# All tiles of u and 13 groups of x turned by DMA transposes in a fused attention and phase-mixing kernel

## The chip, the cores and the metric

One core of one Trainium2 chip runs the kernel. A core has five engines with a queue of their own each: TensorE (PE), VectorE (DVE), ScalarE (ACT), GpSimd (POOL) and SyncE (SP), which only issues DMAs here. Transfers run on 16 DMA engines. The metric is device time in microseconds (us) of one execution, as the median of three runs.

## The reference

Inputs are q, k and v of shape (8, 8, 576, 64): batch, heads, sequence, head dimension. The sequence is cut into nine chunks of 64, and attention runs inside a chunk only. Its output x, (8, 576, 512), goes through a phase layer:

```python
scores = scale * np.matmul(q_c, k_c.transpose(0, 1, 2, 4, 3))      # per chunk of 64
attn = softmax(scores)
x = np.matmul(attn, v_c)                     # to (8, 576, 512), heads side by side
theta = x @ w_theta                          # 512 x 512
zr, zi = x * cos(theta), x * sin(theta)
y = einsum('ts,bsd->btd', w_tok_r, zr) + einsum('ts,bsd->btd', w_tok_i, zi)   # 576 x 576 each
u = x + y
out = u + np.maximum(u @ w_ch, 0.0)          # w_ch 512 x 512, float32
```

## The kernel before

The eight batches are taken in four pairs (0 to 3). A pair has nine tiles of 128 tokens: four of its first batch, four of its second, and one, the middle tile, that holds the last 64 tokens of both. So there are 36 tiles, numbered 00 to 38 in the order by pair and tile (the pair's digit, then 0 to 8). Loads and attention work in groups: A and B are tiles 0, 1 and 2, 3 of the pair's first batch, C and D the same of the second, M is the middle tile alone. Every group but M has two tiles.

The whole program is one list, ORDER, of steps such as `W.02.0`: kind, pair with group or tile, and a slot (a PSUM bank, or the number of a buffer). The steps are emitted in that order, and each engine runs its own instructions in the order in which they were emitted; the engines keep apart only by semaphores where data or a buffer requires it. So a step's place in the list fixes only what stands before it on its own engine. The kinds are:

- `qk`, `v`, `lw`, `lc`: loads that GpSimd issues and that cast to float16 on the way (q and k of a group, v of a group, one block of both token matrices, w_ch). `hq`, `hk`, `lt`: loads in float32 that SyncE issues, with a cast by `cqa`, `ckv`, `cta`. q, k and the weights land in 13 `land` buffers; v lands in `v16`, which holds two pairs.
- `T`, `Tq`, `Tk`, `Tk0`, `Tk1` (VectorE): turn q and k in 32 by 32 blocks. `S` (TensorE): scores. `E` (ScalarE): exp. `V0`, `V1` (TensorE): attention times v, four heads each. `N0`, `N1` (VectorE): division, which writes x.
- `X` (TensorE, through PSUM) with `xa` or `xv` (a copy by ScalarE or VectorE), or `xd` alone (a DMA transpose that SyncE issues): x turned, which `H` needs. `H` (TensorE): theta. `G` (ScalarE): cos and sin. `Z` (VectorE): zr and zi.
- `TW` with `twv` or `twa`: one block of the token matrices turned. `Y`, or in parts `Ya`, `Yb`, `Ym` (TensorE): the mix of all nine tiles of a pair into one output tile. `A` (VectorE): u = x + y, written over x.
- `U` (TensorE, through PSUM) with `ua` or `uv`, or `ud` alone (a DMA transpose that SyncE issues): u turned, which `W` needs. `W` (TensorE): u times w_ch. `R` (VectorE): relu and sum. `st`, `sa`: the store, issued by SyncE or by ScalarE.
- `dm.n.b`: n matmuls on zeros in the early part, with no use of their result.

A transposing matmul of `X` is line 419 and one of `U` line 539, four for each tile; the DMA transposes are line 436 (`xd`) and line 547 (`ud`). The mix is line 522, theta line 457, W line 562, scores line 339, attention line 382, the block transpose of VectorE line 321. An `xd` of a two-tile group moves 256 KB, one of an M group and a `ud` 128 KB. The transposed tiles of u go through eight `uT` buffers and those of x through four `xT` buffers; a DMA transpose waits on SyncE's queue until its input is written and the last reader of its buffer is done, and what stands behind it on that queue waits with it.

Of the kernel before, what the change touches and what calls it, by code (L numbers as in the profile page):

```python
# [65 lines left out]


@with_exitstack
def kernel(
# [86 lines left out]
    def dummies(n, b):  # L156
        for _ in range(n):
            nc.tensor.matmul(banks(b), zeros[:, 0:P], zeros)

    def load_qk(p, g, slot):
# [3 lines left out]
        for w, ap in enumerate((q, k)):  # L166
            if bb is None:
                for b in range(2):
                    nc.gpsimd.dma_start(
                        t[quarter[b], w].rearrange("p h s d -> p h (s d)"),  # L170
                        ap[2 * p + b, :, s0:S, :].rearrange("h (p s) d -> p h (s d)", s=2),
                    )
            else:
                nc.gpsimd.dma_start(  # L174
                    t[:, w].rearrange("p h s d -> p h (s d)"),
                    ap[2 * p + bb, :, s0 : s0 + GT, :].rearrange(
                        "h (p s) d -> p h (s d)", s=2
                    ),
                )
# [55 lines left out]
    def cast_v(engine):  # L235
        def cast(p, g):
            slot = (p % 2) * NT + GROUPS[g][0]
# [421 lines left out]
```

## Time and profile before

| | |
|---|---|
| three runs | 193.11, 193.46, 195.17 us; median 193.46 |
| the profiled execution | 192.63 us, span 190.9 us |
| granted TensorE clock | 0.999 |
| busy: PE, DVE, ACT, POOL | 179.3, 136.8, 100.7, 84.9 us |
| loads by GpSimd | 15.49 MB as landed, in 75152 packets, last issue at 107.33 us |
| DMA transposes | 18 of u, 7 of x; the first issued at 104.68 us |

The time is that of the whole execution; the span is from the first to the last instruction in the trace, and the traced times count from its start. A busy matmul is no proof of a full array, since matmuls are pipelined: a 128x512 one takes 379 ns from start to end, and they follow each other every 216 ns. In the DMA view a line of a queue gives its packets, its megabytes, and the summed time of its packets as a share of 16 engines' time; the packets of one engine overlap, so the share can pass 100%.

### The profile page before, as it was taken

What the parts mean: (1) busy time and instruction counts of PE and PEld (TensorE: products, weight loads), DVE (VectorE), ACT (ScalarE), POOL (GpSimd) and SP (SyncE); (2) the same over time, 40 slices, a digit from 0 to 9 for tenths busy, and PEclk for the clock granted to TensorE, in tenths of its full rate; (3) what the DMA queues carried; (4) which work ended last, traced back from release to release, by engine and by line L of the source; (5) the groups of instructions that cost most, each with busy time, mean ns of one, the idle gap of its engine ahead of it and who ended that gap; (6) DMA issues with size and microseconds to landing.
All of it is one profiled execution on the core that took longest, in us unless ns stands there. A gap on an engine that the chain in (4) does not pass through costs nothing.

```text
span 190.9 us, 6053 instructions
## 1 busy us (share of the span) xinstructions
PE 179.3 (94%) x2626; PEld 93.0 (49%) x2626; DVE 136.8 (72%) x254; ACT 100.7 (53%) x129; POOL 84.9 (44%) x119
## 2 busy tenths in 40 slices
PE   7769899999999999998999999999989999999980
PEld 2245555655556555655456555454544444444430
DVE  0167889789958989959788798967771963672761
ACT  3238979399579780499062774996344650000000
POOL 7786988559856997789578400000000000000000
PEclk9999999999999999999999999999999999999999
DMA  5999999999999999999999998632498315256596
GB/s 156 252 225 187 176 172 174 193 132 159 259 199 162 120 162 198 183 173 194 201 228 200 176 163 180 85 86 82 84 87 177 99 55 137 59 192 165 133 319 213
DMA packets 99867, 31.48 MB, mean 165 GB/s; under 512 B 90880, under 2 KB 94848, under 8 KB 99840
## 3 DMA queue, kind: packets, MB, share of 16 engines
q0 software_dynamic: 75152, 15.49, 93.9%
q1 hardware_dynamic: 21936, 10.75, 24.8%
q10 hardware_dynamic: 2752, 4.85, 7.4%
q8 instruction: 20, 0.33, 0.7%
q14 instruction: 7, 0.06, 0.1%
HBM read 33.06 MB, written 9.44 MB: 223 GB/s over the span
## 4 chain that ended last, share of the span: by engine, by line
PE 64%; DMA 17%; POOL 6%; ACT 5%; DVE 3%; issue 3%; DVEq 0%; POOLq 0%
PE psum L522 29%; DMA land<-in_k_dram 15%; PE psum L562 12%; PE psum L457 11%; PE psum L339 4%; POOL v L214 3%; PE psum L382 2%; POOL land L174 2%; DMA uT<-x 2%; PE psum L419 2%; PE psum L539 2%; ACT L144 1%; PE psum L288 1%; DVE T L321 1%; ACT sin L476 1%
## 5 line engine op out<-in xcount | busy, mean ns | idle before, releaser
L522 PEld LDWEIGHTS <-wT 128*128 128x128 f16 (+1 forms) x360 | 31.0, 100 | 34.5 <-issue 1.2
L214 POOL DMA_DIRECT2D v<-in_v_dram x56 | 42.0, 772 | 7.1 <-DMA land<-in_k_dram 4.0
L522 PE MATMUL psum<-zr,wT 128*128 128x512 f16 (+1 forms) x180 | 44.7, 380 | 0.0
L522 PE MATMUL psum<-zi,wT 128*128 128x512 f16 (+1 forms) x180 | 42.9, 379 | 0.0
L534 DVE TENSOR_TENSOR x<-psum,x 128x512 f16<-128x512 f32 x36 | 24.3, 684 | 20.2 <-PE psum L522 20.0
L562 PE MATMUL psum<-wch,uT 128*128 128x512 f16 (+1 forms) x148 | 35.2, 374 | 1.2 <-DMA uT<-x 0.7
L457 PE MATMUL psum<-wtheta,xT 128*128 128x512 f16 x144 | 34.1, 379 | 0.2 <-DVE xT L442 0.2
L321 DVE STREAM_TRANSPOSE T<-land 128x1024 f32<-128x1024 f32 (+4 forms) x27 | 25.4, 953 | 10.0 <-DMA land<-in_q_dram 5.9
L574 DVE SCALAR_TENSOR_TENSOR o<-psum,x 128x512 f32<-128x512 f32 (+1 forms) x37 | 24.1, 670 | 9.3 <-PE psum L562 9.2
L365 ACT ACTIVATE eT<-psum 128x1024 f16<-128x1024 f32 (+1 forms) x22 | 18.2, 860 | 22.7 <-PE psum L339 20.3
L476 ACT ACTIVATE cos<-psum,pihalf 128x1024 f16<-128x1024 f32 (+1 forms) x22 | 21.1, 958 | 12.5 <-PE psum L457 11.4
L399 DVE TENSOR_TENSOR x<-psum,recip 128x512 f16<-128x512 f32 (+1 forms) x40 | 25.5, 638 | 1.4
L144 ACT ACT_TABLE_LOAD x20 | 25.7, 1283 | 1.1 <-PEq L643 0.7
L562 PEld LDWEIGHTS <-uT 128*128 128x128 f16 x148 | 13.6, 98 | 15.8 <-DMA uT<-x 1.5
L457 PEld LDWEIGHTS <-xT 128*128 128x128 f16 x144 | 13.5, 98 | 16.0 <-DVE xT L442 0.6
L476 ACT ACTIVATE sin<-psum 128x1024 f16<-128x1024 f32 (+1 forms) x22 | 19.0, 865 | 0.0
L174 POOL DMA_DIRECT2D land<-in_q_dram x15 | 14.3, 950 | 5.8 <-DMA land<-in_k_dram 2.1
L339 PE MATMUL psum<-T 32*64 32x64 f16 x1152 | 13.7, 193 | 3.3 <-DVE T L321 3.3
L339 PEld LDWEIGHTS <-T 32*64 32x64 f16 x1152 | 11.8, 106 | 7.6 <-DVE T L321 4.3
L174 POOL DMA_DIRECT2D land<-in_k_dram x15 | 13.6, 907 | 1.7 <-DMA land<-in_k_dram 1.5
L492 DVE TENSOR_TENSOR zr<-x,cos 128x1024 f16<-128x1024 f16 (+1 forms) x18 | 11.2, 623 | 1.3 <-ACT cos L476 1.0
L493 DVE TENSOR_TENSOR zi<-x,sin 128x1024 f16<-128x1024 f16 (+1 forms) x18 | 11.3, 627 | 0.8 <-ACT sin L476 0.7
(39 smaller groups left out, 124.9 us busy)
## 6 DMA issues: line engine op xcount, KB each, us to landing
...
v<-in_v_dram POOLq DMA_DIRECT2D x40, 64.0 KB, 6.4
...
```

The source lines that it names most:

```text
L144: nc.scalar.activation(out=first, in_=pihalf, func=func)
L174: nc.gpsimd.dma_start(t[:, w].rearrange("p h s d -> p h (s d)"), ap[2 * p + bb, :, s0 : s0 + GT, :].rearrange("h (p s) d -> p h (s d)", s=2),)
L214: nc.gpsimd.dma_start(v16[rows, slot + t, :, 0:D], v[b, :, t0 : t0 + m, :].rearrange("h s d -> s h d"),)
L321: nc.vector.transpose(to.bitcast(FP32).rearrange("p (x l s) -> p x s l", l=32, s=2), src.bitcast(FP32).rearrange("p (x s d) -> p x s d", s ...
L339: nc.tensor.matmul(ps[half[r ^ cc], r, h - hs[0]], t[quarter[c], 1, h, :, e], t[quarter[c], 0, h, :, e], start=(e == 0), stop=(e == 1), ti ...
L399: nc.vector.tensor_tensor(out=x.rearrange("p r (h d) -> p r h d", h=H // 2), in0=ps[:, :, :, 0:D], in1=recip[:, 0:n].broadcast_to((P, n, H ...
L457: nc.tensor.matmul(ps[:, (j - js[0]) * DM : (j - js[0] + 1) * DM], xT[:, j, a, :], wtheta16[:, a, :], start=(a == 0), stop=(a == NDB - 1),)
L476: nc.scalar.activation(out=t[:, js[0] : js[-1] + 1].rearrange("p j e -> p (j e)"), in_=ps, func=AF.Sin, bias=bias, scale=1.0,)
L522: nc.tensor.matmul(ps[half[c]] if j == MID else ps, wT[:, kt, t0 : min(t0 + P, S)], z, start=(b is not None and i == 0), stop=(i == len(kt ...
L534: nc.vector.tensor_tensor(out=x, in0=st.pop(("ps_y", p, j)), in1=x, op=ALU.add)
L562: nc.tensor.matmul(ps, uT[:, a, :], wch16[:, a, cols[f]], start=(a == 0), stop=(a == NDB - 1),)
L574: nc.vector.scalar_tensor_tensor(out=o, in0=ps, scalar=0.0, in1=st["x", p][:, j, cols[f]], op0=ALU.max, op1=ALU.add,)
```

## The change

The list ORDER is another one. All 36 tiles of u are turned by `ud`, where 18 were turned by `U` with a copy; 13 of the 20 groups of x are turned by `xd` (1A, 1M, 1C, 2A, 2B, 2M, 2C, 2D and all of pair 3), where seven were. The loads, the stores and all other steps stand in another order, the first group is 0A, whose q and k SyncE loads, and there are 42 dummy matmuls instead of 32. Of the 49 DMA transposes 19 stand in the list ahead of `V1.2D`, the first use of the 42nd of the 45 loads of that list.

Around it, the places of the tiles in x, zr, zi and v16 are worked out by new helpers (`place`, `pairs`, `places`, `middle`), which with the constants given (`WITH_NEXT` empty, `OWN` zero) leave each step one pair's group and the same number of instructions as before, and the tile of zeros shrinks to 128 columns, with the dummies' moving operand broadcast from one column.

```diff
 ORDER = """
-pre.00 qk.0M.0 hq.0A.1 cqa.0A.2 hk.0A.3 Tq.0M.0 Tk.0M v.0M init.00 v.0A dm.21.7 S.0M.0
-E.0M.0 lw.02.4 qk.0B.5 dm.3.7 V1.0M.1 lw.01.6 v.0B ckv.0A lw.00.7 qk.0C.8 Tq.0A.1 Tk0.0A
-Tk1.0A dm.1.7 S0.0A.2 S1.0A.4 E0.0A.1 lw.03.9 v.0C qk.0D.10 v.0D E1.0A lc.00 qk.1A.11
-v.1A N1.0M dm.1.7 V0.0A.6 N0.0A V0.0M.0 V1.0A.1 N1.0A dm.3.5 TW.02.3 lt.00.12 X0.0A.5
-lt.01.1 twv.02 X1.0A.6 xv0.0A.0 cta.01 xv1.0A cta.00 dm.2.7 H0.0A.7 Tq.0B.2 Tk0.0B
-Tk1.0B N0.0M H1.0A.1 S1.0B.2 G0.0A.0 G1.0A Z0.0A dm.1.7 S0.0B.4 Z1.0A TW.01.6 X.0M.0
-Ya.02.1 xv.0M.1 twv.01 E0.0B.2 V0.0B.4 N0.0B qk.1M.0 E1.0B V1.0B.6 N1.0B H.0M.0 Ya.01.2
-X0.0B.3 X1.0B.4 TW.00.5 xv0.0B.2 G.0M.1 xa1.0B H0.0B.7 H1.0B.0 Tq.0C.0 G0.0B.2 G1.0B
-Tk.0C S.0C.3 twv.00 Ya.00.7 Z0.0B TW.03.5 Z1.0B Z.0M Yb.02 Ym.02 E.0C.3 Yb.00 Ym.00 A.02
-Yb.01 Tq.0D.1 V1.0C.3 twa.03 A.00 V0.0C.0 Ym.01 Ya.03.5 Tk.0D N1.0C S.0D.6 U.02.3 N0.0C
-ua.02.0 qk.1B.3 Yb.03 v.1M lw.04.2 X.0C.4 A.01 U.01.0 Ym.03 qk.1C.1 U.00.1 v.1B E.0D.0
-A.03 V1.0D.2 N1.0D ua.01.1 qk.1D.4 qk.2M.12 v.1D V0.0D.6 xa.0C.3 v.2D qk.2C.5 v.1C
-W.02.0 N0.0D H.0C.4 U.03.2 ua.00.2 G.0C.0 T.1A.2 W.00.3 R.00.0 X.0D.1 S.1A.6 xv.0D.0
-E.1A.1 v.2B qk.2A.6 W.01.3 H.0D.4 v.2M V0.1A.6 R.02.1 V1.1A.0 R.01.2 Ym.07.3 uv.03.3
-G.0D.2 Ym.06.2 Z.0C N1.1A Ya.07 Ym.04.0 Ya.04 Ya.06 N0.1A W.03.1 X.1A.6 xa.1A.1 Z.0D
-Yb.06 T.1M.0 Yb.04 TW.04.4 R.03.3 twa.04 T.1B.1 S.1M.7 st.02 E.1M.2 A.04 A.06 S.1B.0
-Yb.07 H.1A.4 V1.1M.6 qk.3M.7 qk.2B.8 v.2A A.07 N1.1M E.1B.3 V1.1B.2 st.01 V0.1B.0 N0.1B
-Y.08.7 V0.1M.6 N1.1B G.1A.1 U.06.0 ua.06.4 Ym.05.1 N0.1M X.1B.4 st.00 U.04.5 Ya.05
-U.07.2 X.1M.3 xa.1B.2 A.08 T.1D.2 xv.1M.3 ua.04.5 H.1B.6 H.1M.0 v.3A qk.3A.9 ua.07.6
-W.07.4 qk.3B.10 T.1C.0 G.1B.0 v.2C S.1C.2 S.1D.5 U.08.7 Yb.05 Z.1A Z.1B G.1M.2 Z.1M
-uv.08.7 R.07.4 Y.12.0 E.1D.0 Y.11.7 v.3M A.12 E.1C.1 A.05 qk.3C.11 V0.1D.4 T.2M.1
-V1.1D.2 V0.1C.0 Y.13.6 N1.1D W.08.2 N0.1D U.12.3 N0.1C A.11 X.1D.4 R.08.5 st.03 uv.12.0
-T.2A.0 Y.10.5 A.10 A.13 V1.1C.0 S.2M.7 v.3C qk.2D.0 S.2A.2 N1.1C U.11.5 st.07 uv.11.2
-W.06.6 st.08 X.1C.0 W.04.1 xa.1D.0 H.1D.4 E.2A.3 E.2M.2 R.04.1 U.05.2 xa.1C.1 T.2B.2
-G.1D.1 H.1C.0 uv.05.1 T.2C.1 W.05.3 Z.1D st.04 R.05.2 S.2B.4 V1.2M.7 G.1C.0 Z.1C V0.2M.2
-E.2B.0 sa.05 N1.2M W.11.3 U.10.0 ua.10.3 Y.17.1 N0.2M R.11.0 R.06.3 A.17 Y.15.7 V0.2B.4
-V0.2A.2 A.15 N0.2B N0.2A V1.2B.0 Y.18.6 A.18 S.2C.4 sa.11 X.2M.7 xv.2M.2 W.10.2 N1.2B
-R.10.4 E.2C.1 T.3M.0 H.2M.3 Y.16.6 U.13.7 G.2M.2 X.2B.4 V1.2A.0 A.16 st.06 st.10 uv.13.6
-xa.2B.3 V0.2C.2 V1.2C.5 N1.2A N1.2C N0.2C W.13.7 R.13.5 sa.13 X.2A.4 xd.2C.0 xv.2A.1
-H.2B.0 U.18.5 U.17.6 U.16.2 uv.16.7 U.15.3 Y.14.7 ua.18.4 T.2D.2 Z.2M ua.17.5 ua.15.1
-W.16.4 H.2A.5 G.2B.1 S.3M.2 S.2D.0 Z.2B G.2A.0 W.12.3 E.3M.2 R.16.1 A.14 Z.2A U.14.4
-W.18.7 R.12.2 R.18.0 Y.21.5 Y.23.6 E.2D.0 st.18 V0.2D.2 T.3C.1 A.21 ua.14.2 v.3B T.3A.0
-V1.2D.0 qk.3D.3 N1.2D N0.2D T.3B.2 sa.12 S.3A.4 W.14.7 sa.16 A.23 xd.2D.2 H.2C.0 E.3A.3
-R.14.3 Y.22.4 G.2C.2 V0.3M.5 V1.3M.2 T.3D.0 A.22 Z.2C N1.3M st.14 S.3B.6 E.3B.1 S.3C.0
-H.2D.3 E.3C.0 N0.3M W.15.6 Y.20.7 v.3D G.2D.1 ud.23.3 R.15.4 V0.3B.0 V0.3A.5 V1.3A.2
-Z.2D A.20 W.17.4 R.17.5 N0.3B Y.24.7 Y.27.4 N1.3A N0.3A A.27 V1.3B.0 xd.3M.3 N1.3B st.15
-A.24 V1.3C.2 N1.3C S.3D.5 Y.28.4 V0.3C.0 ud.20.6 E.3D.2 V0.3D.5 V1.3D.2 A.28 H.3M.7
-N0.3C N0.3D N1.3D xd.3A.1 G.3M.0 ud.27.7 W.27.4 Y.25.0 xd.3B.0 H.3A.5 A.25 ud.22.0
-Y.26.1 G.3A.2 H.3B.2 ud.21.4 st.17 A.26 R.27.0 xd.3C.2 G.3B.1 H.3C.5 Z.3A W.21.7 xd.3D.3
-Z.3M ud.24.2 G.3C.2 Z.3B R.21.2 Z.3C H.3D.0 Y.33.4 W.24.2 Y.31.3 sa.21 R.24.1 A.33
-G.3D.0 Z.3D Y.32.5 st.27 Y.34.6 A.34 Y.36.7 st.24 ud.25.1 W.25.0 A.32 A.36 ud.33.5
-W.33.1 ud.26.7 R.33.3 W.20.2 W.23.4 W.26.6 A.31 R.23.4 R.25.5 ud.32.4 W.32.5 Y.30.7
-sa.23 R.20.0 Y.38.1 Y.35.3 ud.34.2 sa.25 R.26.2 R.32.1 W.34.4 A.30 sa.20 A.35 st.26
-ud.28.1 ud.36.5 W.28.0 R.34.4 ud.30.6 ud.35.3 A.38 W.30.2 R.30.5 R.28.0 Y.37.6 A.37
-sa.33 W.35.5 ud.31.7 ud.38.4 R.35.2 sa.30 sa.28 sa.34 W.36.7 R.36.3 ud.37.2 sa.35 sa.36
-W.31.3 R.31.5 W.38.4 R.38.0 W.22.1 R.22.4 sa.31 sa.32 sa.22 W0.37.2 R0.37.2 W1.37.0
-st.38 R1.37.3 sa1.37 st0.37
+pre.00 hq.0A.0 hk.0A.1 cqa.0A.2 ckv.0A Tq.0A.0 Tk0.0A dm.23.7 S0.0A.0 Tk1.0A lt.00.3
+lt.01.4 init.00 v.0A qk.0M.5 E0.0A.0 S1.0A.2 E1.0A cta.01 dm.3.7 V1.0A.4 cta.00 N1.0A
+V0.0A.6 N0.0A dm.8.3 X0.0A.0 X1.0A.1 Tq.0M.1 xv0.0A.0 xa1.0A qk.0B.6 dm.1.7 H0.0A.2 v.0M
+Tq.0B.2 v.0B H1.0A.3 Tk.0M Tk1.0B S.0M.4 lw.02.7 qk.0C.8 E.0M.1 S1.0B.5 lw.00.9 Tk0.0B
+S0.0B.0 E0.0B.2 V0.0M.7 E1.0B N0.0M dm.1.4 V1.0M.4 N1.0M dm.1.1 V1.0B.0 N1.0B dm.1.7
+X.0M.7 xv.0M.1 G0.0A.0 V0.0B.5 G1.0A N0.0B lw.03.10 dm.2.4 TW.02.0 Z1.0A dm.1.7 X0.0B.4
+xv0.0B.2 X1.0B.7 xa1.0B H.0M.2 Z0.0A v.0C H1.0B.5 H0.0B.6 Tq.0C.0 twa.02 G.0M.1 Tk.0C
+dm.1.7 S.0C.3 Z.0M qk.0D.11 G0.0B.2 G1.0B Z0.0B Z1.0B Ya.02.7 TW.00.0 TW.03.5 twv.03
+twv.00 Yb.02 Ym.02 Ya.03.2 E.0C.3 Ym.07.5 V1.0C.3 N1.0C Tq.0D.1 V0.0C.0 Ya.00.6 Yb.00
+Tk.0D S.0D.3 E.0D.0 Ym.00 N0.0C A.02 A.00 X.0C.0 xa.0C.3 v.0D lw.01.12 Yb.03 qk.1A.0
+V0.0D.3 V1.0D.6 Ym.03 N0.0D N1.0D H.0C.0 X.0D.3 xv.0D.0 TW.01.6 H.0D.3 qk.1M.1 G.0C.0
+A.03 T.1A.2 S.1A.0 twa.01 Ya.01.2 T.1M.0 Z.0C S.1M.6 G.0D.1 E.1M.1 Ym.06.7 Yb.01 E.1A.2
+qk.1B.2 v.1M Ya.07 Z.0D Yb.07 v.1A V0.1A.3 V1.1A.0 qk.1C.4 v.1B T.1B.1 N1.1A lw.04.3
+A.07 lc.00 Ya.06 qk.1D.5 V1.1M.6 Yb.06 N1.1M S.1B.0 N0.1A Ym.05.5 Ya.05 E.1B.3 Ym.01
+Ym.04.6 A.01 v.2A V0.1M.3 qk.3M.6 V0.1B.0 N0.1B T.1C.2 ud.00.0 N0.1M ud.03.1 v.1C v.1D
+qk.2A.7 Ya.04 qk.3C.8 v.2M Yb.04 A.04 qk.2M.9 qk.2B.10 qk.2D.11 v.2B ud.02.2 Yb.05
+V1.1B.0 N1.1B A.06 ud.07.3 W.00.4 W.03.2 X.1B.3 xa.1B.1 R.03.0 qk.3A.12 v.2C qk.2C.0
+v.3M S.1C.0 W.07.6 T.1D.0 qk.3B.1 R.07.1 E.1C.0 v.3A W.02.7 TW.04.2 H.1B.0 v.3B v.2D
+R.02.2 xd.1A.2 A.05 G.1B.2 twv.04 H.1A.6 R.00.3 T.3M.1 xd.1M.3 H.1M.5 Y.08.2 Z.1B G.1A.0
+sa.03 Z.1A ud.01.4 sa.02 V0.1C.3 V1.1C.0 st.07 G.1M.1 Z.1M S.1D.6 Y.10.5 N0.1C A.08 A.10
+E.1D.2 N1.1C Y.12.3 T.2A.2 V1.1D.6 st.00 V0.1D.4 N1.1D N0.1D Y.11.2 A.11 A.12 W.01.0
+R.01.4 ud.04.5 Y.13.1 S.2A.6 E.2A.1 X.1D.4 v.3D T.2M.0 S.2M.5 A.13 S.3M.2 V0.2A.0 N0.2A
+V1.2A.6 xa.1D.0 ud.08.6 N1.2A xd.1C.1 H.1D.3 G.1D.2 ud.06.7 H.1C.0 W.04.6 ud.05.0 W.08.7
+G.1C.0 E.3M.3 W.05.3 ud.10.1 ud.12.3 T.2B.2 S.2B.0 ud.13.2 Z.1D R.04.5 Z.1C W.10.4
+R.05.1 Y.14.6 T.2D.0 sa.04 R.10.3 E.2B.0 sa.05 V0.2B.2 N0.2B sa.10 V1.2B.0 E.2M.2 N1.2B
+V0.2M.4 st.01 Y.15.5 Y.17.2 R.08.0 V1.2M.3 Y.16.0 A.15 N0.2M A.17 N1.2M T.2C.1 A.16
+W.12.1 T.3A.2 A.14 R.12.2 S.2C.4 E.2C.1 sa.12 Y.18.7 A.18 xd.2A.2 V0.2C.2 xd.2B.3 T.3C.1
+V1.2C.4 S.2D.0 E.2D.0 H.2A.6 N0.2C T.3B.0 H.2B.0 qk.3D.2 N1.2C G.2A.1 xd.2M.0 H.2M.2
+Z.2A G.2B.2 Z.2B G.2M.0 Z.2M W.06.3 W.13.4 ud.14.4 W.14.5 R.14.5 v.3C S.3B.6 R.13.4
+V1.2D.0 Y.22.2 R.06.1 N1.2D E.3B.2 Y.23.5 st.08 V0.3B.6 V1.3B.3 A.22 sa.13 ud.16.5
+T.3D.0 V0.2D.0 N0.2D Y.21.2 N0.3B A.23 Y.20.0 W.16.1 A.20 R.16.3 xd.2C.1 H.2C.6 st.06
+xd.2D.2 H.2D.0 G.2C.1 ud.11.6 N1.3B A.21 Z.2C W.11.5 G.2D.2 R.11.2 ud.15.0 W.15.3 Z.2D
+S.3D.6 S.3A.4 S.3C.0 Y.26.2 E.3C.1 A.26 st.16 Y.25.0 A.25 R.15.0 E.3A.2 V0.3A.4 st.14
+Y.28.1 N0.3A ud.21.1 ud.23.3 ud.18.7 sa.15 ud.17.2 A.28 V0.3C.2 V1.3C.4 st.11 E.3D.0
+ud.22.4 N0.3C ud.25.5 V1.3A.6 N1.3A W.23.0 W.18.1 R.18.4 R.23.1 N1.3C xd.3A.3 xd.3B.0
+W.17.2 Y.27.3 A.27 R.17.3 V1.3M.6 V1.3D.0 V0.3D.4 N0.3D st.18 ud.26.6 V0.3M.7 W.21.3
+R.21.5 N0.3M sa.21 N1.3M Y.24.2 st.17 H.3B.4 G.3B.0 A.24 N1.3D xd.3C.1 Z.3B W.25.3
+R.25.2 H.3A.6 ud.27.0 W.26.2 G.3A.1 xd.3M.2 H.3M.0 Z.3A G.3M.2 st.25 H.3C.4 W.22.1 Z.3M
+Y.31.3 xd.3D.0 H.3D.6 Y.30.0 G.3C.0 G.3D.1 Z.3C Z.3D A.30 Y.33.4 R.22.0 ud.28.3 A.31
+Y.36.5 A.33 Y.38.6 Y.32.7 A.36 A.38 W.28.0 Y.35.1 Y.34.3 st.23 ud.24.7 R.28.4 ud.33.2
+A.32 W.33.4 ud.31.1 sa.22 ud.20.5 ud.36.6 W.36.5 A.35 A.34 ud.38.4 W.38.6 R.33.3 sa.28
+sa.33 ud.30.3 R.36.5 sa.36 ud.35.2 R.38.2 W.30.0 R.30.1 W.31.7 R.26.0 Y.37.1 W.35.3
+sa.38 ud.34.6 A.37 st.30 R.31.4 W.34.4 R.34.3 sa.31 W.27.5 R.35.5 W.20.6 R.27.2 R.20.1
+ud.32.4 sa.26 W.24.0 sa.34 W.32.2 R.24.4 ud.37.3 sa.20 W0.37.1 W1.37.7 sa.24 R.32.0
+R0.37.3 sa.32 st.35 R1.37.5 sa1.37 st.27 st0.37
 """.split()
+
+
+
+WITH_NEXT = ()
+OWN = 0
...
-    zeros = const.tile([P, DM], FP16, name="zeros")
+    zeros = const.tile([P, P], FP16, name="zeros")
...
     st = {}
     for name in ("x", "zr", "zi"):
-        t = const.tile([P, 2 * NT, DM], FP16, name=name)
-        for p in range(NP):
-            st[name, p] = t[:, p % 2 * NT : (p % 2 + 1) * NT]
+        st[name] = const.tile([P, 2 * NT + OWN, DM], FP16, name=name)
+
+    def place(p, j):
+        return p % 2 * MID + j if j < MID else 2 * MID + (1, 0, 1, 2 * OWN)[p]
+
+    def pairs(p, g):
+        if g != "M":
+            return [p]
+        ps = [p, p + 1] if p in WITH_NEXT else [p]
+        return sorted(ps, key=lambda x: place(x, MID))
...
-            nc.tensor.matmul(banks(b), zeros[:, 0:P], zeros)
+            nc.tensor.matmul(banks(b), zeros, zeros[:, 0:1].broadcast_to((P, DM)))
...
             if engine == "d":
                 nc.sync.dma_start(
                     xT.rearrange("p j a c -> p (j a) c"),
-                    st["x", p][:, j0 + js[0] : j0 + js[-1] + 1].rearrange("p j d -> p (j d)"),
+                    st["x"][:, j0 + js[0] : j0 + js[-1] + 1].rearrange("p j d -> p (j d)"),
                     transpose=True,
                 )
...
             if engine == "d":
-                nc.sync.dma_start(uT, st["x", p][:, j], transpose=True)
+                nc.sync.dma_start(uT, st["x"][:, place(p, j)], transpose=True)
```

More of the change, by code (lines that the diff above doesn't have):

```diff
@@ L157, in dummies, with middle @@
         for _ in range(n):
-            nc.tensor.matmul(banks(b), zeros[:, 0:P], zeros)
+            nc.tensor.matmul(banks(b), zeros, zeros[:, 0:1].broadcast_to((P, DM)))
+    def middle(p, g):
+        return [2 * x + b for x in pairs(p, g) for b in range(2)]
     def load_qk(p, g, slot):
@@ L167, in load_qk @@
             if bb is None:
-                for b in range(2):
+                for i, b in enumerate(middle(p, g)):
                     nc.gpsimd.dma_start(
-                        t[quarter[b], w].rearrange("p h s d -> p h (s d)"),
-                        ap[2 * p + b, :, s0:S, :].rearrange("h (p s) d -> p h (s d)", s=2),
+                        t[quarter[i], w].rearrange("p h s d -> p h (s d)"),
+                        ap[b, :, s0:S, :].rearrange("h (p s) d -> p h (s d)", s=2),
                     )
@@ L207, in load_v @@
         j0, bb, s0 = GROUPS[g]
-        slot = (p % 2) * NT + j0
+        slot = places(p, g)[0]
         if bb is None:
-            parts = [(half[b], 0, 2 * p + b, s0, CH) for b in range(2)]
+            parts = [
+                (half[i // 2 ^ i % 2], i // 2, b, s0, CH) for i, b in enumerate(middle(p, g))
+            ]
         else:
@@ L236, in cast @@
         def cast(p, g):
[L237 removed]
+            slot = places(p, g)[0]
             to, fro = v16[:, slot : slot + 2, :, 0:D], st.pop(("v32", p, g))
@@ L397, in divide @@
             nc.vector.reciprocal(out=recip[:, 0:n], in_=ps[:, :, :, D : D + 1])
-            x = st["x", p][:, j0 : j0 + n, f * DM // 2 : (f + 1) * DM // 2]
+            x = st["x"][:, slice(*places(p, g)), f * DM // 2 : (f + 1) * DM // 2]
             nc.vector.tensor_tensor(
@@ L406, in norm, with tiles @@
         return divide
-    def tiles(g, i):
-        return range(size(g)) if i is None else [i]
+    def tiles(p, g, i):
+        return range(size(p, g)) if i is None else [i]
     def x_t(i):
         def products(p, g, b):
-            js = tiles(g, i)
-            j0 = GROUPS[g][0]
+            js = tiles(p, g, i)
+            j0 = places(p, g)[0]
             ps = banks(b, 1, FP16)[:, 0 : len(js) * DM]
@@ L429, in copy @@
         def copy(p, g, slot=None):
-            js = tiles(g, i)
-            j0 = GROUPS[g][0]
+            js = tiles(p, g, i)
+            j0 = places(p, g)[0]
             if slot is not None:
@@ L451, in products @@
         def products(p, g, b):
-            js = tiles(g, i)
+            js = tiles(p, g, i)
             ps = banks(b, len(js))
@@ L469, in put @@
         def put(p, g, slot=None):
-            js = tiles(g, i)
+            js = tiles(p, g, i)
             ps = st.pop(("ps_t", p, g, i))
@@ L484, in turn @@
         def turn(p, g):
-            j0, bb, s0 = GROUPS[g]
+            j0, j1 = places(p, g)
             cos, sin = st["trig", p, g]
-            x, zr, zi = st["x", p], st["zr", p], st["zi", p]
-            if bb is not None:
-                js = tiles(g, i)
+            x, zr, zi = st["x"], st["zr"], st["zi"]
+            if g != "M":
+                js = tiles(p, g, i)
                 fro = slice(js[0], js[-1] + 1)
@@ L532, in add_x @@
     def add_x(p, j):
-        x = st["x", p][:, j]
+        x = st["x"][:, place(p, j)]
         nc.vector.tensor_tensor(out=x, in0=st.pop(("ps_y", p, j)), in1=x, op=ALU.add)
@@ L538, in u_t @@
         for a in range(NDB):
-            nc.tensor.transpose(ps[:, a, :], st["x", p][:, j, a * P : a * P + P], id16)
+            nc.tensor.transpose(ps[:, a, :], st["x"][:, place(p, j), a * P : a * P + P], id16)
         st["ps_uT", p, j] = ps
@@ L574, in last @@
             nc.vector.scalar_tensor_tensor(
-                out=o, in0=ps, scalar=0.0, in1=st["x", p][:, j, cols[f]],
+                out=o, in0=ps, scalar=0.0, in1=st["x"][:, place(p, j), cols[f]],
                 op0=ALU.max, op1=ALU.add,
```

39 lines of the change are left out of this document (20 added, 19 removed).

## The prediction

> **What bounds the kernel now.** I read the page first: the span, the busy shares, the row of TensorE in 40 slices, the DMA row.
>
> ```profile
> span 190.9 us, 6053 instructions
> ...
> PE 179.3 (94%) x2626; PEld 93.0 (49%) x2626; DVE 136.8 (72%) x254; ACT 100.7 (53%) x129; POOL 84.9 (44%) x119
> ...
> PE   7769899999999999998999999999989999999980
> ...
> PEclk9999999999999999999999999999999999999999
> DMA  5999999999999999999999998632498315256596
> ...
> q0 software_dynamic: 75152, 15.49, 93.9%
> ```
>
> TensorE is full from the fifth slice almost to the end, at the full clock. The DMA row is full too, up to about 115 us, and what fills it are the loads that GpSimd issues (q0). So two things are saturated for the first 60% of the span. The chain of waits, in order of time, says which of them ends last in the middle:
>
> ```profile
> 68.94 0.78 POOL land L174
> 69.73 7.27 DMA land<-in_k_dram
> ...
> 77.76 6.11 DMA land<-in_k_dram
> ...
> 83.97 0.50 DVE T L321
> ```
>
> The chain runs through the loads of group 2A (landed at 69.73 + 7.27 = 77.00) and group 2B (83.87), and VectorE turns 2B's keys the moment they are there. The last such place is 2D, in VectorE's timeline:
>
> ```profile
> 107.06 1.25 DVE L321 STREAM_TRANSPOSE T<-land 128x1024 f32<-128x1024 f32 x1 [0.67 <-DMA land<-in_k_dram]
> ```
>
> VectorE stood idle 0.67 us for it. So up to 107 us the loads arrive just in time, and TensorE's work fits behind them; from there on TensorE alone sets the pace. A stream with no slack is what this change adds to.
>
> **The gain.** The build of the changed kernel has 112 transposing matmuls fewer: 72 of line 539 (18 tiles of u) and 40 of line 419 (groups 1A, 1C, 2A, 2B of x, and 1M, 2M). Prices, with those of the work that stays, from the chain:
>
> ```profile
> 35.47 0.64 PE psum L339 x64
> ...
> 38.18 0.22 PE psum L539 x4
> 38.41 0.38 PE psum L382 x32
> ...
> 42.57 0.45 PE psum L419 x8
> ...
> 151.99 1.73 PE psum L457 x8
> ...
> 156.53 7.77 PE psum L522 x36
> 164.30 5.18 PE psum L562 x24
> ```
>
> 18 x 0.22 + 5 x 0.45 = 6.2 us of TensorE go (the two M groups make one full one). The PSUM copies of the same tiles go too (ScalarE and VectorE); neither engine bounds, so they count nothing. Ten more dummy matmuls (42 for 32), all before the loads bind, count nothing either; nor do the smaller zeros tile and the renumbered places of x, zr, zi and v, which move no more data. TensorE's first rows:
>
> ```profile
> 1.19 7.18 PE L158 MATMUL psum<-zeros 128*128 128x512 f16 x21 [1.19 <-DVE pihalf L149]
> 10.87 0.70 PE L339 MATMUL psum<-T 32*64 32x64 f16 x32 [2.50 <-DVE T L321]
> ```
>
> The new start (group 0A first, loaded by SyncE, behind 23 dummies) moves the first useful matmul from 10.87 us to 1.19 + 23 x 7.18 / 21 = 9.1; it does not bring the load stream forward, which both kernels start at once, so I count it nothing as well.
>
> **The cost.** In the order, 19 transposes (13 of u, four of two-tile x groups, two of M groups) stand ahead of the use of v.2D and are issued while loads are queued. The kernel before has one transpose in that condition, xd.2C (from SyncE's timeline):
>
> ```profile
> 104.68 1.34 SPq L436 DMA_TRANSPOSE xT<-x  x1
> ```
>
> Two windows of the DMA view, 98 to 104 us (loads and one 256 KB store) and 109 to 114.2 us (loads, one store and this transpose's packets):
>
> ```profile
> q0 software_dynamic: 4613, 0.89, 176.6%
> q1 hardware_dynamic: 134, 0.25, 12.4%
> ...
> q0 software_dynamic: 2039, 0.35, 99.7%
> q1 hardware_dynamic: 1056, 0.26, 56.4%
> q10 hardware_dynamic: 144, 0.26, 14.2%
> ```
>
> Without it 4613 load packets go in 6 us, 769 in each us; with it 2039 go in 5.2 us, where 3998 would have gone. The 1959 missing packets are 2.55 us of the stream. The loads were all issued by then, so they did not lack orders; and the last ones landed late (window 104.6 to 115.8 us, then the page's median of the same kind):
>
> ```profile
> v<-in_v_dram POOLq DMA_DIRECT2D x2, 64.0 KB, 9.7
> xT<-x SPq DMA_TRANSPOSE x1, 9.9
> ...
> v<-in_v_dram POOLq DMA_DIRECT2D x40, 64.0 KB, 6.4
> ```
>
> So a two-tile transpose takes its whole time away from the loads: **2.5 us**. For one tile of u there is no such row. Alone (window 163.7 to 167 us, two of them):
>
> ```profile
> DMA  0000000000000016999998520000001799999841
> ...
> q1 hardware_dynamic: 1080, 0.26, 39.1%
> uT<-x SPq DMA_TRANSPOSE x2, 2.4
> ```
>
> Each fills the engines for about ten slices of 0.083 us, 0.8 us; by summed packet time 0.391 x 3.3 / 2 = 0.65. The bounds are 0.65 and half of the two-tile price, 1.27; I take **0.8**, nearest to the row of the same operation. An M group moves as many packets as a tile of u: 0.8. For the two-tile one the bounds are 1.3 (twice 0.65) and 2.55. Sum: 13 x 0.8 + 4 x 2.5 + 2 x 0.8 = 22.0 us of the stream, between 15.0 and 29.3.
>
> The Trainium skill ("DMA: Bandwidth & Descriptors", § Latency and other measured facts) gives DMA transposes an effective 261 GB/s: by that, an estimate, 0.5 us for the 128 KB of a u tile and 1.0 for 256 KB, and a sum of 11.5 us instead of 22.0, and a time of 194 us. The one measured under loads took 2.55, so here the trace disagrees with the page.
>
> Two things give some of it back. The stream has gaps that more packets can fill: those in which GpSimd waited for compute.
>
> ```profile
> POOL land L174 <- DVE x L399: 1.4, 2, 1.1
> ...
> POOL v L214 <- PE psum L382: 1.0, 1, 1.0
> ...
> POOL land L174 <- DVE o L574: 0.9, 1, 0.9
> ...
> POOL land L174 <- DVE uT L549: 0.5, 1, 0.5
> POOL v L214 <- PE psum L522: 0.5, 1, 0.5
> ...
> POOL land L174 <- DVE recip L397: 0.5, 1, 0.5
> ```
>
> These are 4.8 us, in which other loads were still in flight: between 0 and 4.8, I take 2.4. And by v.2D the new order has nine stores where the old one had twelve before T.2D: three stores, 0.5 us each (0.124 x 6 = 0.74 by packet time in the window above, less overlap), 1.5.
>
> **The sum.** The end is set by v.2D's landing: of the loads in the new order it is the last with little work of TensorE between its place in the stream and its use. Up to v.2D the new order has loaded everything but v.3D, qk.3D and v.3C; up to qk.2D the old one had loaded everything but v.3B, v.3D and qk.3D: the same amount, and it had landed at 107.0. So v.2D lands at 107.0 + 22.0 - 2.4 - 1.5 = 125.1 us. TensorE's queue cannot pass V1.2D; behind it stand, by the order, 18 whole mixes (9 matmuls of 0.216 each, 34.9), 23 W (0.86, 19.9), 6.5 thetas of two tiles (1.73, 11.2), 3 scores (1.9) and 12 halves of attention, two of M (4.2): 72.1 us. To the end of the span another 4.8 us, as before:
>
> ```profile
> 183.36 2.77 PE L562 MATMUL psum<-wch,uT 128*128 128x512 f16 x16 [0.71 <-DMA uT<-x]
> ```
>
> (183.36 + 2.77 = 186.1, and 190.9 - 186.1 = 4.8.) With 0.2 from landing to matmul: 125.1 + 0.2 + 72.1 + 4.8 = **202.2 us of span**. The profiled execution took 192.63 us, 1.7 over its span, and the median of the three runs is 0.8 above that: 202.2 + 2.5 = **204.7 us**. TensorE first meets the late loads near V1.1B, and the delay grows up to V1.2D; the 6.2 us saved lie in that stretch and are waited away. With all bounds at one end: 107.0 + 15.0 - 4.8 - 1.5 gives 195 us, 107.0 + 29.3 - 1.5 gives 214, and 216 without the stores' share. Behind 126 us the remaining transposes find no loads, land 2.4 us after issue as in the row above, and have 2 to 30 us of TensorE work between their input and their use; I count them nothing. If this cover failed at the end, the wait of 0.71 us before the last W is what it cost already.
>
> **Rivals.**
>
> *The transposes fit beside the loads.* They read and write on-chip memory only, and the load packets' summed time is 176.6% of the window, so that the engines hold more than one packet at a time. Then v.2D lands by 106 us, and only TensorE's saving counts: 190.9 - 6.2 = 184.7, with 2.5 outside: **187 us**, faster. It decides where the transposes cost the stream less than 4.5 us in all (107.6 - 107.0 + 2.4 + 1.5, with 107.6 = 184.7 - 77.1), a fifth of my prices; at half of them the kernel is about as fast as before. Against it stands the pair of windows; for it, that they show one transpose only, at the end of the stream.
>
> *Only the landing gets late.* The loads keep pace, but SyncE's transposes land 10 us or more after issue, and the six x groups reach theta late. By the sums of the order TensorE has 10.2 to 14.5 us of work between attention and theta of 1A, 1M, 1C, 2B and 2M; normalising comes first:
>
> ```profile
> L399 DVE TENSOR_TENSOR x<-psum,recip 128x512 f16<-128x512 f32 (+1 forms) x40 | 25.5, 638 | 1.4
> ```
>
> With 0.64 us for it, about as much for the two hand-overs (an estimate) and 9.9 of landing, a group needs 11.2 us: 2M is over by 1. With a landing of 12 four are over, by 0.5 to 3, some 6 in all; with 14, some 12. So 187.2 + 1 to 12, **188 to 199 us**, 194 in the middle.
>
> *The waits switch the clock down.* At the start, in the row above, 21 dummies took 7.18 us where 21 x 0.216 = 4.5 is the pace later. 2.65 us is the price of one cold start. If TensorE stands still for several us before V1.2D, as in my forecast, it pays this once behind the last wait: **207 us**. The Trainium skill ("TensorE: Matmul & The Clock Gate", § Part 1) puts the switch at an idle window of about 3.4 us; before, no gap after the start was longer than 2.5 us, and no run here shows one yet.
>
> **How the numbers follow.** Forecast 0.62 (205 us, own range 195 to 216), with the clock in addition 0.14 (207), landing alone 0.09 (194), no cost 0.15 (187). The range runs from 190 to 216: it leaves out the case without cost and the outer edge of the clock's. A measurement of this kernel tells about 1% from no change, so slower is above 195.4: 0.62 + 0.14 + half of 0.09, less the low edge of the forecast, 0.79; within 1%: 0.05; faster: 0.16.
>
> **What the next profile would show.** Right: the DMA row full to 130 us or more; q1's packets in the slices of the loads; VectorE's T and TensorE's scores and attention of 1B to 2D waiting for DMA, some 15 us in all; TensorE's row with 5s to 8s between 45 and 125 us; V1.2D near 125 us and some 72 us of dense work behind it. PEclk below 9 in that stretch would show the clock. Wrong: loads done by 116 us with transposes among them; waits on xT or uT ahead of those on land and v.

## The result and the profile after

The changed kernel takes 215.41 us (median of four, 214.57 to 222.3) where the kernel before took 194.31 on the same chip: a ratio of **1.109** (1.103 to 1.115). The direction was right and 215.4 lies just inside the range (190 to 216). The size was not: 204.7 was forecast, +5.8% on the median then shown, and +10.9% was measured. The profiled execution took 215.17 us with a span of 213.4, so the step from span to time (1.8) is as before, and the miss of 11.2 us (213.4 - 202.2) is in the span. Executions more than 1.5% above the fastest of the same kernel (here that of 222.3 us) are left out of every ratio and of the times compared below, where this kernel counts with 215.2 us; the traces of e6 and e9 are of such executions.

The page of the kernel after, its span, busy shares, three of the rows by 40 slices of 5.3 us, and two queues:

```profile
span 213.4 us, 5858 instructions
...
PE 186.2 (87%) x2524; PEld 91.7 (43%) x2524; DVE 132.5 (62%) x243; ACT 84.2 (39%) x104; POOL 84.2 (39%) x119
...
PE   8769999999699989099891799999699999999990
...
PEclk9958999999999999859999599999699999999999
DMA  6999999999999999999999999956414865045886
...
q0 software_dynamic: 75152, 15.49, 93.9%
q1 hardware_dynamic: 36736, 13.90, 34.2%
```

The DMA row is full for 26 slices, to about 138 us, where it was full to 115. The loads are the same 75152 packets; q1, which had 21936 packets, has 36736. TensorE's row has holes that were not there (0 at about 85 us, 1 at about 115), and the clock row, all nines before, has three dents behind the start: at about 91, 120 and 152 us.

TensorE's timeline names the holes (start, duration, then in brackets the idle time before and what ended it), and the waits by engine sum them up (us, times, longest):

```profile
90.39 1.92 PE L359 MATMUL psum<-T 32*64 32x64 f16 x64 [5.39 <-DVE T L341]
...
118.88 1.07 PE L359 MATMUL psum<-T 32*64 32x64 f16 x64 [5.85 <-DVE T L341]
...
151.61 0.31 PE L359 MATMUL psum<-T 32*64 32x64 f16 x5 [1.96 <-issue]
```
```profile
DVE T L341 <- DMA land<-in_k_dram: 18.3, 7, 6.4
...
PE psum L359 <- DVE T L341: 12.5, 4, 5.9
```

The scores of 2M and of 2C wait 5.4 and 5.9 us for VectorE's turn of the keys, and that waits for their load: 18.3 us of VectorE's waiting for keys in all, where the forecast had "some 15". The third wait, 1.96 us inside the scores of 3C (3D, 3A and 3C run in a row, 64 matmuls each, and 187 were done), is for nothing that the profile shows.

What the waits do to the clock, in the table of stretches (length; busy time of PE, PEld, DVE, ACT, POOL; granted clock; DMA share; GB/s):

```profile
85.00:90.00 5.00, 0.00 (x0) 0.00 (x0) 1.32 (x2) 2.92 (x4) 4.72 (x7) 0.96 1.59 151
90.00:97.00 7.00, 6.61 (x108) 3.85 (x109) 3.52 (x7) 0.55 (x1) 2.35 (x3) 0.54 1.87 146
...
118.90:123.80 4.90, 4.90 (x82) 2.34 (x82) 2.83 (x4) 1.02 (x1) 3.75 (x7) 0.50 2.25 161
...
151.10:154.50 3.40, 2.89 (x12) 1.16 (x13) 0.00 (x0) 1.94 (x2) 0.00 (x0) 0.50 0.43 120
```

After each of the three waits TensorE works at half clock for some 3 to 6 us.

The chain that ended last, in order of time:

```profile
87.61 16.75 DMA v<-in_v_dram
...
105.77 11.72 DMA land<-in_k_dram
...
117.58 1.26 DVE T L341
...
118.88 1.07 PE psum L359 x50
119.95 3.96 PE psum L540 x18
...
132.67 0.25 PE psum L401 x16
...
147.45 2.19 PE psum L359 x187
149.65 1.96 issue
```

Up to 117.5 us it consists of loads; the last one is 2C's keys, landed at 105.77 + 11.72 = 117.49. From there TensorE alone runs to the end: 18 matmuls of a mix in 3.96 us (half pace), V1.2D at 132.6, and the odd wait at 149.65.

### The profile page after: what moved, and what is told of

Its sections match the earlier page's. It is cut to its first block, busy times and chain, and to the rows that moved or that the text cites. A ratio compares the mean times of both kernels' runs of the same rounds, so it can differ in the third digit from the quotient of the medians.

```text
span 213.4 us, 5858 instructions
## 1 busy us (share of the span) xinstructions
PE 186.2 (87%) x2524; PEld 91.7 (43%) x2524; DVE 132.5 (62%) x243; ACT 84.2 (39%) x104; POOL 84.2 (39%) x119
## 3 DMA queue, kind: packets, MB, share of 16 engines
q0 software_dynamic: 75152, 15.49, 93.9%
q1 hardware_dynamic: 36736, 13.90, 34.2%
## 4 chain that ended last, share of the span: by engine, by line
DMA 44%; PE 37%; POOL 10%; issue 4%; DVE 1%; ACT 1%; DVEq 0%; ACTq 0%; POOLq 0%
DMA land<-in_k_dram 30%; PE psum L540 18%; DMA v<-in_v_dram 12%; PE psum L580 9%; PE psum L475 7%; POOL v L234 5%; POOL land L192 4%; PE psum L359 2%; DMA xT<-x 1%; PE psum L401 1%; DVE T L341 1%; ACT cos L494 1%; POOL land L271 1%; ACT eT L385 0%; DVE o L592 0%
## 5 line engine op out<-in xcount | busy, mean ns | idle before, releaser
L540 PE MATMUL psum<-zr,wT 128*128 128x512 f16 (+1 forms) x180 | 47.2, 399 | 1.0 <-DVE x L417 1.0
L540 PE MATMUL psum<-zi,wT 128*128 128x512 f16 (+1 forms) x180 | 44.6, 395 | 0.0
L341 DVE STREAM_TRANSPOSE T<-land 128x1024 f32<-128x1024 f32 (+4 forms) x27 | 25.0, 950 | 18.3 <-DMA land<-in_k_dram 18.3
L475 PE MATMUL psum<-wtheta,xT 128*128 128x512 f16 x144 | 35.1, 394 | 0.7 <-DVE o L592 0.4
L580 PE MATMUL psum<-wch,uT 128*128 128x512 f16 (+1 forms) x148 | 33.9, 374 | 0.2 <-DVE x L552 0.2
L359 PE MATMUL psum<-T 32*64 32x64 f16 x1152 | 15.4, 198 | 14.6 <-DVE T L341 12.5
L359 PEld LDWEIGHTS <-T 32*64 32x64 f16 x1152 | 13.3, 111 | 20.5 <-DVE T L341 15.6
L580 PEld LDWEIGHTS <-uT 128*128 128x128 f16 x148 | 14.1, 98 | 16.0
L415 DVE RECIPROCAL recip<-psum 128x8 f32<-128x8 f32 (+1 forms) x40 | 7.6, 191 | 14.9 <-PE psum L401 14.1
L192 POOL DMA_DIRECT2D land<-in_q_dram x15 | 13.6, 908 | 5.6 <-DMA land<-in_k_dram 2.1
L401 PE MATMUL psum<-v,eT 64*64 64x65 f16 x576 | 11.5, 200 | 4.9 <-DMA v<-in_v_dram 3.2
```

What stands on the lines that cost most here:

```text
L192: nc.gpsimd.dma_start(t[:, w].rearrange("p h s d -> p h (s d)"), ap[2 * p + bb, :, s0 : s0 + GT, :].rearrange("h (p s) d -> p h (s d)", s=2),)
L341: nc.vector.transpose(to.bitcast(FP32).rearrange("p (x l s) -> p x s l", l=32, s=2), src.bitcast(FP32).rearrange("p (x s d) -> p x s d", s ...
L359: nc.tensor.matmul(ps[half[r ^ cc], r, h - hs[0]], t[quarter[c], 1, h, :, e], t[quarter[c], 0, h, :, e], start=(e == 0), stop=(e == 1), ti ...
L475: nc.tensor.matmul(ps[:, (j - js[0]) * DM : (j - js[0] + 1) * DM], xT[:, j, a, :], wtheta16[:, a, :], start=(a == 0), stop=(a == NDB - 1),)
L540: nc.tensor.matmul(ps[half[c]] if j == MID else ps, wT[:, kt, t0 : min(t0 + P, S)], z, start=(b is not None and i == 0), stop=(i == len(kt ...
L580: nc.tensor.matmul(ps, uT[:, a, :], wch16[:, a, cols[f]], start=(a == 0), stop=(a == NDB - 1),)
```

## The experiments

**Is it the transposes?** e1 replaces the 19 early transposes by VectorE copies that don't transpose (so the transposing of these tiles is left out) and keeps the order. e2 does that too and issues the 19 transposes all the same, into spare tiles that nobody reads.

```diff
 # e1: of line 565 (and 454) for the 13 tiles and 6 groups ahead of V1.2D
-nc.sync.dma_start(uT, st["x"][:, place(p, j)], transpose=True)
+nc.vector.tensor_copy(out=uT.rearrange("p a c -> p (a c)"), in_=st["x"][:, place(p, j)])
 # e2: in addition
+nc.sync.dma_start(spare, st["x"][:, place(p, j)], transpose=True)
```

> The changed kernel with its 19 early DMA transposes (13 of u, 6 of x) left out: VectorE copies those tiles untransposed into the same buffers, so W and theta of them work on wrong operands, and every other step stands. Theory (the transposes' packets take their time from the loads): without them group 2C's keys land near 96 us instead of 117.5, TensorE has no long wait, and the time is 186 to 190 us. Rival (the transposes cost nothing, the new order is slow by itself): 212 us or more.

> As the run of copies alone, but the 19 transposes are issued too, into four spare tiles that nobody reads: the traffic without anybody waiting for its landing. Theory (traffic slows the loads): 211 to 217 us, as the changed kernel. Rival (only the landing is late, and W and theta wait for it): 187 to 191 us, as the copies alone.

e1 took 204.27 us, a ratio of 1.047 (1.041 to 1.054): neither theory. e2 took 215.16, 1.107 (1.098 to 1.116), the time of the changed kernel, as its theory said. So what the transposes cost is their traffic. In e2 nothing waits for their landing, and the scores of 2C begin at 118.6 us as in the changed kernel (118.9). The load queue between 60 and 100 us, in the changed kernel and then in e1:

```profile
q0 software_dynamic: 18841, 3.79, 134.0%
q1 hardware_dynamic: 6992, 2.38, 43.5%
...
uT<-x SPq DMA_TRANSPOSE x8, 8.6
```
```profile
q0 software_dynamic: 25966, 5.20, 153.4%
q1 hardware_dynamic: 432, 0.79, 5.9%
...
land<-in_k_dram POOLq DMA_DIRECT2D x7, 256.0 KB, 7.9
```

In 40 us 7125 load packets fewer go, 11.0 us at e1's 649 per us, for 6560 packets more on q1. A tile of u has some 540 of these (23 tiles' worth in 19 transposes make up the 12384 between the page's 36736 above and e1's 24352): **0.9 us a tile**. 2C's keys, issued in e1 by

```profile
90.64 0.89 POOL L194 DMA_DIRECT2D land<-in_k_dram  x1
```
```profile
land<-in_k_dram POOLq DMA_DIRECT2D x1, 256.0 KB, 6.9
```

landed at 97.5 us, 20.0 earlier than in the changed kernel. v.2D landed at 109.5 where it landed at 128.5: 19.0. But only 11 of these 20 us reach the end (215.16 - 204.27), because e1 loses something else: it has the transposing matmuls of 28 tiles fewer on TensorE than the kernel before, loads that come early, and is still 9 us slower; that is taken up below, with the waits for "issue".

**The price of a tile, twice more.** e3 issues the 13 early transposes of u twice; e7 adds 13 transposes into spare tiles to the kernel before, beside its first 13 U steps, and e8 does the same with plain copies of as many bytes.

```diff
 # e3, behind the transpose of an early tile
+nc.sync.dma_start(spare, st["x"][:, place(p, j)], transpose=True)
 # e7, behind a U step of the kernel before
+nc.sync.dma_start(spares[:, next(spare) % 3], st["x", p][:, j], transpose=True)
 # e8 instead
+nc.sync.dma_start(spares[:, next(spare) % 3], st["x", p][:, j].rearrange("p (a c) -> p a c", c=P))
```

> The changed kernel with each of the 13 early transposes of u issued twice, the second time into spare tiles. Theory with 1.0 us of the load stream for each (as the packets of the profile after suggest): 12 of them stand before the landing of 2C's keys, so 12 us more, 227 us; with the 0.8 us of the prediction 225 us. Rival (landing alone, 1.2 us of SyncE's queue for each, mostly hidden): 215 to 219 us.

> The kernel before with 13 DMA transposes added, one beside each of its first 13 transposes of u by TensorE, into spare tiles that nobody reads; nothing else moves. Theory (1.05 us of the load stream for each, and in this order the loads bind at 2A, 2B and 2D): 12 to 13 of them stand ahead of the last binding load, 12 to 14 us more, 206 to 209 us, and up to 4 more if the clock drops. Rival (they fit beside the loads): 193 to 196 us.

> As the run before this one, but the 13 added transfers are plain DMA copies of the same 128 KB, in 128 packets of 1 KB instead of 512 of 256 bytes. If the price goes by packets: a fourth to a half, 3 to 6 us more than the kernel before, 197 to 201 us. If it goes by bytes or by transfer: as with the transposes, 206 to 209 us. If nothing but the transposing costs: 193 to 196 us.

e3: 227.2 us, 12.0 more than the changed kernel for 13 tiles, 0.92 each. e7: 206.7 (205.32 and 208.01), ratio 1.068 (1.058 to 1.079), some 13 us for 13 tiles, 1.0 each, in a kernel whose order is untouched. Both came as their theory said. e8: 195.84, ratio 1.012 (1.010 to 1.015), 2 us or a little more, under 0.2 each: inside its third case, though not quite nothing. Queue q1 in the kernel before, in e7 and in e8:

```profile
q1 hardware_dynamic: 21936, 10.75, 24.8%
```
```profile
q1 hardware_dynamic: 29008, 12.46, 31.0%
```
```profile
q1 hardware_dynamic: 23808, 12.46, 27.6%
```

That is 544 packets a tile in e7 and 144 in e8, for the same 1.71 MB. So the price is that of the transposing with its many small packets, not of moving 128 KB within the chip.

**Is it the clock?** e4 puts 22, 24 and 8 dummy matmuls ahead of the scores of 2M, 2C and 3C, so that TensorE does not stand still; e5 puts a mix between the two scores at 149 us.

```diff
 # e4
-T.2M.0 S.2M.5 ... R.12.2 S.2C.4 ... S.3A.4 S.3C.0
+T.2M.0 dm.22.5 S.2M.5 ... R.12.2 dm.24.4 S.2C.4 ... S.3A.4 dm.8.2 S.3C.0
 # e5
-S.3D.6 S.3A.4 S.3C.0 Y.26.2
+S.3D.6 S.3A.4 Y.26.2 S.3C.0
```

> The changed kernel with dummy matmuls in its three longest waits of TensorE: 22 ahead of the scores of 2M, 24 ahead of those of 2C, 8 ahead of those of 3C. Theory with the clock: the granted clock stays at 1.0 there, the half-speed stretches of 118.9 to 123.8 and 151.1 to 154.5 us go (2.4 and 1.7 us; the one behind 2M is waited away), 210 to 212 us. Without the clock as a cause: 215 us or more by the dummies that outlast the waits.

> The changed kernel with two neighbouring steps exchanged: the mix of tile 26 runs ahead of the scores of 3C, so that no longer three groups of scores (384 instructions of TensorE in 2.2 us) run back to back. Theory (TensorE's wait of 1.96 us at 149.65 us is for its next block of instructions, and the half-speed stretch behind it follows from that wait): both go, 2.0 + 1.7 us less, 211 to 212 us. Rival (it waits for ScalarE or a bank): 214 to 216 us.

Both missed: 215.6 us in e4 (214.85 and 216.33) and 214.96 in e5 (ratio 1.110, 1.105 to 1.115), no gain over 215.2. In both a local effect came. In e4 the stretch behind the wait for 2C ran at full clock (that behind 2M did not: 3.79 us of the wait were left there); in e5 the wait and the dent at 150 us are gone. But each found another wait, in e4 and then in e5:

```profile
123.98 0.35 PE L359 MATMUL psum<-T 32*64 32x64 f16 x19 [2.12 <-issue]
```
```profile
96.10 4.85 PE L475 MATMUL psum<-wtheta,xT 128*128 128x512 f16 x11 [3.34 <-issue]
...
131.62 0.29 PE L401 MATMUL psum<-v,eT 64*64 64x65 f16 x13 [2.10 <-DMA v<-in_v_dram]
```

e5 shows that v.2D binds 2 us behind 2C: what is gained ahead of V1.2D is waited away there. And both have a wait of 2 to 3 us ended by "issue", in the middle of a step whose operands are long there.

**What is this "issue"?** e1 has three of them, and a half clock at the start:

```profile
56.09 0.25 PE L403 MATMUL psum<-v,eT 64*64 64x65 f16 x7 [1.00 <-issue]
...
89.23 3.61 PE L482 MATMUL psum<-wtheta,xT 128*128 128x512 f16 x11 [3.52 <-issue]
...
140.69 0.24 PE L361 MATMUL psum<-T 32*64 32x64 f16 x5 [1.82 <-issue]
```
```profile
12.00:19.00 7.00, 6.38 (x50) 3.10 (x50) 3.82 (x8) 2.54 (x3) 6.40 (x9) 0.51 1.85 157
```

They stand ahead of TensorE's matmuls number 863, 1375 and 2143 of the trace, those of the changed kernel ahead of 863 and 2143, those of e4 and e5 ahead of 863, 1759 and 1375. The differences are multiples of 128 matmuls, and a matmul with its weight load is two instructions. A queue of its own carries packets of 16 KB, about one for each 256 of TensorE's instructions; the changed kernel between 148 and 151 us:

```profile
q1 hardware_dynamic: 1051, 0.26, 53.3%
q8 instruction: 1, 0.02, 2.4%
```

So TensorE may wait for its next block of instructions. The traces of all thirteen kernels bear this out: they have 21 waits of TensorE longer than 0.5 us that are ended by "issue", all on this grid of 128 matmuls (three, all in the order before, one matmul off it), and each ended 1.3 to 1.6 us after a packet of this queue had landed. The packet in the window above took from 149.08 to 150.23 us, and TensorE went on at 151.61. If that is the cause, the waits belong to counts, not to steps. e9 is e1 with 56 matmuls more ahead of everything (70 very small ones for 14 of the dummies at the start); e10 is the changed kernel with the same; e11 is e9 with dummies moved into TensorE's wait at 10 us.

```diff
 # e9, e10
-dm.23.7 S0.0A.0
+ds.70.7 dm.9.7 S0.0A.0     # ds: n matmuls of eight columns of zeros
 # e11, in addition
-dm.3.7 V1.0A.4 ... dm.8.3 X0.0A.0
+dm.10.7 V1.0A.4 ... dm.2.3 X0.0A.0
```

> The kernel with copies in place of the 19 early transposes (transposing of these tiles left out), and 70 very small matmuls in place of 14 of the 23 dummies at the start, so that TensorE's list has 56 matmuls (112 instructions) more ahead of everything. Theory: TensorE's waits that the trace gives to nothing (1.0, 3.5 and 1.8 us ahead of matmuls 863, 1375 and 2143) are waits for the next block of 256 instructions; they lie at fixed counts, so none stands ahead of the same matmuls of the program any more: those three places run through, and waits of 1 to 3 us come up at most where a block is short, which by the counts is inside the scores that were at 110 and at 138 us. The end then moves by no more than some 3 us either way from 202.2. Rival: the waits belong to the steps (a buffer, a bank, a semaphore that the trace doesn't show); then they stand ahead of the same matmuls as before, with the same lengths.

> The changed kernel with the same 56 matmuls more ahead of everything. Theory: the 1.96 us ahead of the scores at 151.6 us is a wait for instructions; it goes from that place, and one of 1 to 2 us comes up some 56 matmuls earlier, inside the scores at 147.4 to 149.6, since that block is just as short; the time stays within 2 us of 215.4. Rival: it belongs to the scores' banks or inputs; then it stays ahead of the same matmuls.

> The same as the shifted kernel with copies, with seven dummies more ahead of the first attention matmuls (10 instead of 3) and six fewer behind it (2 instead of 8), which fill TensorE's wait of 2 us for v at 10.4 us. Theory that the half clock at the start of the new order (12.0 to 18.8 us) is part of what the order loses by itself: the spell goes, and the end comes 2 to 4 us earlier than in the shifted kernel. Rival: the stretch up to 37 us is bound by loads, and the end stays within 1 us of it.

e9: 199.6 us, ratio 1.027 (1.021 to 1.033), against e1's 1.047 (1.041 to 1.054): by the ratios 4 us earlier than e1, more than expected, by instructions that compute nothing. e11 took 197.28 and 194.50 us in two executions, which is too few for an interval. The waits of the first of these, and its start:

```profile
105.56 0.44 PE L365 MATMUL psum<-T 32*64 32x64 f16 x30 [2.32 <-issue]
...
115.23 1.89 PE L595 MATMUL psum<-wch,uT 128*128 128x512 f16 x4 [3.08 <-DVE uT L576]
```
```profile
12.00:19.00 7.00, 5.63 (x117) 2.75 (x118) 4.54 (x10) 2.37 (x4) 6.56 (x10) 0.97 1.93 168
```

None of e1's three places waits any more (above 0.5 us); the one wait left to "issue" is ahead of matmul 1759, again 128 x 3 before 2143, and inside the scores of 2D that were at 110 us in e1, one of the two places foretold. In e9's own trace the waits stand ahead of matmuls 351, 1375 and 1759, on the grid too and not on e1's steps. The rival (waits of the steps) falls. The second place foretold, the scores at 138 us, stayed without a wait, so the count says where a wait can be, not that it comes. The wait of 3.08 us is for a copy that only these kernels have. The half clock at the start has not gone in e11, as its theory had it, but come earlier and shorter: from 9.0 to 12.4 us, where e1 has it from 12.0 to 18.8.

e10: 213.25 us, ratio 1.101 (1.094 to 1.109), which is not to be told from the changed kernel's. Its 1.96 us at 151 are gone, and none came up 56 matmuls earlier. Yet 2C still binds:

```profile
117.90 1.07 PE L363 MATMUL psum<-T 32*64 32x64 f16 x64 [3.19 <-DVE T L345]
```

Its scores begin at 117.9 us for 118.9: the load stream decides, and the time that TensorE gains ahead of it is spent waiting there.

**The early transposes back on TensorE**, in the changed order:

```diff
-ud.00.0 ud.03.1 ... xd.1A.2 xd.1M.3 ... ud.14.4
+U.00.4 ua.00.0 U.03.2 uv.03.1 ... X.1A.7 xa.1A.2 X.1M.6 xa.1M.3 ... U.14.3 ua.14.4
```

> The changed kernel with its 19 early transposes (13 tiles of u, 6 groups of x) turned by TensorE again, with a copy by ScalarE or VectorE; the other 30 stay DMA transposes. Theory (two causes: the transposes slow the loads by 20 us, of which 11 reach the end, and the rest of the new order loses time of its own): 5.1 us of TensorE more than the run of copies alone and 2 us less of waits for copies, 204 to 208 us. Rival (the transposes are the whole loss, and the copies on VectorE spoiled that run): 188 to 193 us.

226.45 us, ratio 1.169 (1.162 to 1.175): a miss. The loads came early, but the engines wait for each other around the inserted steps, here ScalarE's and VectorE's copies:

```profile
ACT uT L570 <- PE psum L558: 17.4, 7, 4.5
...
DVE uT L568 <- PE psum L558: 16.5, 2, 8.4
```

The order has no room for them where I put them, and the run says nothing of the transposes' own price.

## Why the prediction was right and wrong

- **"A stream with no slack is what this change adds to": right.** e2 has the whole cost with nobody waiting for a landing. The rival that the transposes fit beside the loads fell, and so did the one of late landing alone: the landings did get late (8.5 us in the median for a u tile), but nothing hung on them. The direction alone proves little: e1, without the early transposes, is slower than the kernel before as well.
- **The price of the transposes, 22.0 us: right in sum, wrong in its parts.** u was put at 0.8 and measured 0.9 to 1.0; the two-tile groups have twice the packets of a u tile, so some 1.8 to 2.0 by these runs and not the 2.5 taken from one window (for them alone no run was made). The Trainium skill ("DMA: Bandwidth & Descriptors", § Latency and other measured facts) states 261 GB/s for transposes; 128 KB in 0.92 to 1.0 us are 131 to 142, so with loads queued e3 and e7 show about half of it. The delay of v.2D was 19.0 us where 22.0 - 2.4 = 19.6 were forecast.
- **Where v.2D lands without them: 105.5 forecast (107.0 - 1.5), 109.5 in e1, a term 4.0 us too small.** "The same amount had been loaded" is true of bytes; the new order issues them later (the last load of all goes out at 107.3 us before and at 110.9 in e1). With the transposes v.2D landed at 128.5 for the forecast 125.1, 3.4 us late; V1.2D could have started at 128.7 by it.
- **"The end is set by v.2D's landing": the step that failed.** The load that bound was 2C's keys, at 117.5 us. From its scores (118.9) to V1.2D lie 11.5 us of TensorE's work at full pace, so V1.2D could not start before 130.4, 5.1 us later than the 125.3 of the forecast: 3.4 by the late stream of the point above, and 1.7 because 2C's keys bound and not v.2D. I looked for the load with the least work behind it and checked one; two were nearly equal, as e5 shows, where v.2D binds.
- **"It pays this once behind the last wait": a rival with a chance of 0.14 happened beside the forecast.** After the wait for 2C, TensorE lost 2.2 us at half clock (V1.2D at 132.6 instead of 130.4). The price per cold start, 2.65 us, was right to half a us; to treat it as a separate case was wrong, since a forecast with a standstill of several us contains it. The Trainium skill ("TensorE: Matmul & The Clock Gate", § Part 1) puts the switch at an idle window of about 3.4 us; the dents behind 5.39 and 5.85 us agree with it, the one behind 1.96 us does not.
- **"72.1 us of dense work": 75.9** (208.5 - 132.6; the tail behind it is 4.9 where 4.8 was forecast). 1.96 us are the wait for instructions and some 1.4 the half clock behind it; the rest is small. Neither was in any step.

So 3.4 + 1.7 + 2.2 + 3.8 and 0.1 in the tail are the 11.2 us. What **the new order loses by itself** was put at nothing: the first rival had 187 us for transposes that cost nothing, and e1, without the traffic of the early ones, takes 204.3, which is 9 us more than the kernel before. Other counts of TensorE's instructions, with other dummies at the start, take 4 of these 9 us away in e9, and with dummies in the wait at 10 us some 6 to 9 in the two executions of e11. In the changed kernel such losses are mostly hidden ahead of the loads that bind (e10). The two causes overlap: with instruction blocks shifted, taking the traffic away is worth some 14 us (213.25 - 199.6), without the shift 11. How e1's 9 us divide stays open: e9 changes the dummies at the start along with the count, and the copies of e1, e9 and e11 add waits of their own. In none of these runs is the new order faster than the kernel before, not even with the early transposes left out.
